# A new order of all steps in a fused attention and feed-forward kernel, with one dummy matmul step fewer

## The chip, the core and the metric

The kernel runs on one core of a Trainium2 chip. The metric is the device time of one execution in microseconds. Times of several executions are compared by their median; the profiles show one execution each.

The core has five engines, each with its own queue[...]: TensorE (PE; its weight loads are shown as PEld), VectorE (DVE), ScalarE (ACT), GpSimd (POOL) and SyncE (SP). POOL and SP also issue the transfers.

## The reference

Eight batches of 8 heads, 576 rows and 64 columns go through an attention with exponential features, then through a Fourier mixing and a feed-forward network.

```python
def phi(x):
    proj = np.einsum('bhsd,df->bhsf', x, w_phi)            # 64 -> 128
    proj = proj - np.max(np.abs(proj), axis=-1, keepdims=True)
    return np.concatenate([np.exp(proj), np.exp(-proj)], axis=-1)
q_p, k_p = phi(q), phi(k)
kv = np.einsum('bhsf,bhsd->bhfd', k_p, v);  z = np.sum(k_p, axis=2)
x = einsum('bhsf,bhfd->bhsd', q_p, kv) / (einsum('bhsf,bhf->bhs', q_p, z)[..., None] + 1e-6)
# heads side by side: x is (8, 576, 512)
mixed = np.real(fft(fft(x, axis=1), axis=2))
u = x + mixed
un = (u - mean(u)) / np.sqrt(var(u) + 1e-6)                # over the 512 columns
out = u + np.maximum(un @ w_ch1, 0.0) @ w_ch2              # 512 -> 2048 -> 512
```

## The kernel before, in words

The work of a batch is cut into *streams*, and each stream into *steps*. A stream is a Python generator; each `yield` ends a step. A string `PLAN` of 1239 letters says which stream takes its next step. Instructions are issued in that order, and each engine works through its own in that order, so the string alone sets the order on all five engines. Nothing is scheduled at run time: an engine waits where the operand of its next instruction isn't ready, and everything behind it waits too.

I name a step by its letter, its batch and its number in the stream, counted from 0: S6.3 is step 3 of stream S for batch 6. The letters are:

- K, V, Q: the loads of k, v and q, issued from POOL (`fetch_k`, `fetch_v`, `fetch_q`). V_b.0 loads the last 64 rows, V_b.1 heads 0 to 3 and V_b.2 heads 4 to 7 into the tile VS, of which there is one. B and A: the transposes of k and q on SP (`arrive_k`, `arrive`).
- T (`steps`): products of keys and of queries with w_phi and their exponentials on ACT. T_b.0 to T_b.8 are for the keys, T_b.9 to T_b.17 for the queries. A product of a key or query step (T_b.9, 11, 14, 16) takes a buffer of the pool `pj`, and its second exponential is made in the step after.
- P (`maxima`): the maxima of the queries. R (`kmax`): those of the keys, on DVE. S (`scaled`): exponentials of these maxima on ACT, then multiplications of V with them on POOL (lines 451 and 466): S_b.0 for the last rows, S_b.1 to S_b.4 for two heads each.
- M (`mixing`): M_b.0 to M_b.7 are the products kv, one head each; M_b.8 to M_b.15 the quotients, one head each, partly on DVE and POOL; M_b.16 to M_b.25 the Fourier transforms. D (`folded`): sums and differences on DVE ahead of these transforms.
- N (`normalise`): the normalised rows UN on ACT, and their transposes UT on SP. U (`scales`): the scale 1/sqrt(var).
- F (`forward`): the feed-forward in 68 steps. A hidden step has four matmuls `psf` (line 1222), an output step two `pso` (line 1239). Two hidden steps of the first 256 rows share one ReLU on ACT (the "paired ReLUs", line 1229); those of the other 320 rows have one each (line 1227).
- W loads the two weights, C, H, Z make constants, and G and J transpose the first batch's k and q on TensorE.
- Y (`stir`): four matmuls of ones whose result nobody reads.

Batch 0 uses the same letters in longer forms (`first_features`, `first_heads`), in which the heads go in pairs 0, 3, 2, 1, and its k and q wait in the space of the weights W2b.

Buffers join the streams. `pj` has two PSUM buffers, shared by T, P (from batch 2 on) and M_b.8 to M_b.20; R reads what T has put there; `pb` has three, shared by F and most of M; `pk` has one, for kv and the dummies. A matmul into a buffer waits until the one before it in that buffer was read.

```python
    with tc.manual_schedule():
        count_first()
        load_first()
        count_rest()
        for name in PLAN:
            step(name)
```

Of the kernel before, what the change touches and what calls it, by code (L numbers as in the profile page):

```python
# [20 lines left out]


PLAN = (
    "YYCCYCYGCGZTGRTGZTZTZRZJQQGSTJRKTPYTSTPRYTWJJJRMPTMTSSMTPPSTPTMTZQMTMMTMPMMVKBTCMTMDTYMVHMYYDYYDDAHM"
    "HYYHTHMMMHKMTTRMNMTMYQNNYVMSNTKNMFFNFNRRFSTPFTPTUFWMNFFMNFFSFRTFVMFFTCURPSYUBNTUTFSUFMFQKTFMFTPPMQTP"
    "VMTFFPUTFUMTMFFAFMMTFFMQFMFDFRFMFTVFFFFRFMFTFFMFFPFFTFFFQDDFFFRFMFTKFFDMTFFFFTFMFFMFRTFMRTFMFSSSSTTM"
    "NPFFTNPBTMMMSMQFTMTPPMFFMFFTMFFFPVTAMFFFPNFFMTFFMNNKUMFFVMMFFQTMFFTFRMRFFTFFFQFMFFMFMFFFPTFFRFFFFDFD"
    "VFTPFFFDFFDKTPRFTFFMMTSFFBFFFMMSSFFMFFRTMTMFFTNMSMFFFTNPPMFMTFFFTMTFSTPMFFFMFFQPFTFMFFVFNMFFFMKTFFAM"
    "NNMFFMFUMFVFFMVQFFMFTTRFFMFFFKFRFFMTQFFFDTMRFFFFFDTPFFFTDDFRPFFFFFMTFTFMFFMFBMRFSSMFFTTTMFMTFFFTFNFN"
    "SFMTTMMFFFPMFTMSTPPMFFSMTFFMNFPFMFFPFFVKMNQKFFMNMUFFMFFMFFVMFAFMFQMFFMFTTRFQRFFFTVFMFFFFDFTPFRFFFPDT"  # L30
    "FFFTFFFDFFFDRTMTMFFFFMBFSMFFSMRFTFTTMSFMFTFNMMMTMFTFFFMNFPSSTMTNFFFFTPPMFFFMFTFPQMFVFKFPFFMFFMANMFFN"
    "FFMKFFMFTUTFMFFRFRFFSVFMFFFFFTMFTFQFRMFDVTFFFMTRFFDFFFFFFFDFFDFTMFTBQFMFFMSFMFRFMFTFTTMFFSMTNFTNFFMP"
    "SMFFMMTFMPTFSMTFFMTPFMFTFFQMFNPPPFVMFFAMFFPFNNUMVFMFTFMFMFFFMFRFFMTRTFSFFFFFPFFMFVFMTFFRFFTFDFDFPTFF"
    "FFDDFRFFTTMMFFFFFFMMFRSFTFFMTFTMTFFNTFSMNFFFMTFTTFMFMFMTSPFMFFFFMFFSMFTPPMFFFMFFMNPFMFFPNNFUMMFFFFMF"
    "FMFFFMMFFFFFFMFFMFFFDFFDFFFDFFDFMFFFFMMFMFMFFFMNMFNFFFFFFFFMMFFFFFFFFFFFFFFFFFFFFNMNFNFFFFFUFFFFFFFF"
    "FFFFFFFFFFFFFFFFFFFFFFFFFFFFFFFFFFFFFFF"
)


# [1 line left out]
def kernel(  # L41
# [11 lines left out]
    B, H, S, D = q.shape  # L53
    DF = w_phi.shape[1]
    C = H * D
# [1277 lines left out]
        return run  # L1333

    def stir(b):
        for i in range(16):
            ps = pk.tile([128, 512], F32, tag="pk", name="idle")
            for x in range(4):
                nc.tensor.matmul(  # L1339
                    ps[:], lhsT=ones_b[:], rhs=ones_b[:].unsqueeze(1).to_broadcast([128, 4, 128]),  # L1340
                    start=True, stop=True,
                )
            yield

    def fold_later(b):
# [4 lines left out]
        "U": (scales, 1), "P": (part(0), 7), "T": (part(1), 18), "R": (part(2), 5),  # L1350
        "S": (part(3), 5), "K": (fetch_k, 2), "V": (fetch_v, 3), "Q": (fetch_q, 3),
        "A": (arrive, 1), "B": (arrive_k, 1), "W": (load_ffn_weights, 2),
        "C": (constants, 6), "H": (sines, 6), "Y": (stir, 16), "G": (turn_first_k, 5), "J": (turn_first_q, 5), "Z": (pads, 6),
    }
    LONGER = {("N", 0): 10, ("U", 0): 7, ("M", 0): 24, ("T", 0): 20}
    at_ = {name: (1 if name in "KVBQA" else 0, 0) for name in STREAMS}
# [51 lines left out]
```

## Time and profile before

| what | value |
|---|---|
| median of 4 runs | 429.64 us (426.75 to 429.8) |
| the profiled execution | 426.75 us |
| its span, first to last instruction | 425.0 us |
| TensorE busy | 402.8 us, 95% |
| VectorE busy | 330.8 us, 78% |
| ScalarE busy | 305.3 us, 72% |
| GpSimd busy | 207.0 us, 49% |
| dummy matmuls (line 1339) | 64, 19.2 us busy |
| first feed-forward matmul | 52.4 us |
| mean granted TensorE clock | 0.999 |

All times within the execution are microseconds from the first instruction. The busy share of TensorE counts overlapping and waiting matmuls, so it is not a share of its peak. In the timeline a row gives start, duration, engine, line, operation, output and inputs; square brackets hold the idle time of the engine ahead of it and what ended that. "PEld ... issue" is time in which nothing that the profile shows was waited for.

### The profile page before, as it was taken

To read this page: it belongs to the slowest core of one execution; us is meant where nothing else is said; L and a number is where in the kernel's file an instruction comes from. 1 tells how busy PE (TensorE), PEld (TensorE's weight loads), DVE (VectorE), ACT (ScalarE), POOL (GpSimd) and SP (SyncE) were. 2 spreads that over 40 slices of the span, in tenths; PEclk is the share of its full clock that TensorE was granted. 3 is DMA by queue.
4 is the path that set the end of the run, shared out by engine and by line. 5 is a ranking of instruction groups with operands and counts; after the bars stand their busy time and mean duration, and the time that the engine had idled before them with its cause. 6 is when DMAs were issued, how large, how long until landed. Compare 5 with 4: busy or idle time off the path is not lost.

```text
span 425.0 us, 10430 instructions
## 1 busy us (share of the span) xinstructions
PE 402.8 (95%) x4126; PEld 255.1 (60%) x4126; DVE 330.8 (78%) x682; ACT 305.3 (72%) x626; POOL 207.0 (49%) x271
## 2 busy tenths in 40 slices
PE   8789789998899999999999999999999999999994
PEld 3465466744676558564675558565856567657562
DVE  4879787899789985998879885998899868965302
ACT  5986899747975889488847997688858785454450
POOL 7992588542965292825574274835554333300100
PEclk9999999999999999999999999999999999999999
DMA  8999979995597945994499259695473141104204
GB/s 218 179 177 160 126 81 163 160 132 105 105 129 80 126 76 80 124 124 77 86 147 140 51 81 133 85 116 106 79 93 49 27 88 32 27 0 79 68 23 86
DMA packets 108699, 42.70 MB, mean 100 GB/s; under 512 B 82859, under 2 KB 103595, under 8 KB 108651
## 3 DMA queue, kind: packets, MB, share of 16 engines
q0 software_dynamic: 45936, 16.60, 37.5%
q1 hardware_dynamic: 62479, 25.31, 32.7%
q8 instruction: 32, 0.52, 0.5%
q10 hardware_dynamic: 236, 0.13, 0.1%
q14 instruction: 16, 0.13, 0.1%
HBM read 36.77 MB, written 9.44 MB: 109 GB/s over the span
## 4 chain that ended last, share of the span: by engine, by line
PE 50%; DVE 31%; ACT 15%; issue 2%; DMA 1%; DVEq 0%; POOL 0%; ACTq 0%; SPq 0%
PE psf L1222 16%; PE pso L1239 13%; DVE cb L999 5%; DVE R L903 4%; DVE MK L511 4%; DVE tg L994 4%; PE kv L887 3%; PE pso L1286 2%; DVE CEO L1034 2%; PE idle L1339 2%; DVE MQ L555 2%; PE pu L1104 2%; ACT KPn L497 2%; DVE rd L1001 2%; DVE X L1245 2%; PE psD L1045 2%
## 5 line engine op out<-in xcount | busy, mean ns | idle before, releaser
L1222 PE MATMUL psf<-UT,W1b 128*128 128x320 bf16 (+1 forms) x1024 | 141.3, 286 | 0.8 <-ACT HT L1229 0.4
L1239 PE MATMUL pso<-W2b,HT 128*128 128x512 bf16 x512 | 125.0, 379 | 0.0
L1222 PEld LDWEIGHTS <-W1b 128*128 128x128 bf16 x1024 | 94.4, 98 | 28.3 <-issue 2.9
L1239 PEld LDWEIGHTS <-HT 128*128 128x128 bf16 x512 | 46.0, 98 | 44.8 <-issue 1.4
L1227 ACT ACTIVATE HT<-psf 128x320 bf16<-128x320 f32 x128 | 53.4, 449 | 24.8 <-PE psf L1222 19.3
L1002 POOL TENSOR_TENSOR X<-cb,rd 128x320 f32<-128x320 f32 x56 | 41.4, 742 | 38.0 <-DVE rd L1001 35.5
L466 POOL TENSOR_TENSOR VCn<-VS,VCn 128x512 bf16<-128x512 bf16 x28 | 29.7, 1060 | 41.6 <-ACT VCn L461 33.3
L1229 ACT ACTIVATE HT<-psf 128x512 bf16<-128x512 f32 x64 | 38.4, 600 | 13.3 <-PE psf L1222 13.0
L555 DVE TENSOR_REDUCE MQ<-psq 128x8 f32<-128x1024 f32 (+1 forms) x32 | 34.2, 1085 | 13.8 <-PE psq L547 13.5
L1245 DVE SCALAR_TENSOR_TENSOR X<-pso,rs,X 128x512 f32<-128x512 f32 x32 | 23.5, 736 | 22.0 <-PE pso L1239 21.9
L497 ACT ACTIVATE KPn<-psk 128x1024 bf16<-128x1024 f32 x28 | 28.5, 1019 | 14.2 <-DVE MK L511 14.0
L497 ACT ACTIVATE KPp<-psk 128x1024 bf16<-128x1024 f32 x28 | 28.7, 1026 | 11.1 <-PE psk L491 11.0
L451 POOL TENSOR_TENSOR V4N<-VS,V4N 64x256 bf16<-64x256 bf16 x14 | 8.8, 631 | 53.2 <-ACT V4N L447 48.3
L1094 DVE TENSOR_TENSOR X<-pu,X 128x512 f32<-128x512 f32 (+3 forms) x49 | 23.5, 529 | 13.8 <-PE pu L1104 13.6
L511 DVE TENSOR_REDUCE MK<-psk 128x8 f32<-128x1024 f32 x28 | 33.7, 1206 | 0.1
L1190 POOL TENSOR_TENSOR rs<-VE,mhalf 128x5 f32<-128x5 f32 (+1 forms) x9 | 10.3, 1143 | 41.1 <-DVE VE L1189 41.0
L466 POOL TENSOR_TENSOR VCp<-VS,VCp 128x512 bf16<-128x512 bf16 x28 | 29.7, 1060 | 0.0
L606 ACT ACTIVATE QPHP<-psh 128x1024 bf16<-128x1024 f32 x28 | 28.8, 1028 | 0.5 <-PE psh L597 0.3
L606 ACT ACTIVATE QPHN<-psh 128x1024 bf16<-128x1024 f32 x28 | 28.9, 1034 | 0.0
L1150 ACT ACTIVATE UN<-X,MV 128x512 bf16<-128x512 f32 (+1 forms) x35 | 24.7, 722 | 5.4 <-issue 2.7
L1174 DVE BATCH_NORM_STATS2 st<-X 128x6 f32<-128x512 f32 (+1 forms) x40 | 27.0, 675 | 0.1
L284 POOL DMA_DIRECT2D QS<-in_q_dram x28 | 23.7, 847 | 3.3 <-DMA QT<-QS 3.2
(465 smaller groups left out, 818.8 us busy)
## 6 DMA issues: line engine op xcount, KB each, us to landing
out_dram<-X SPq DMA_DIRECT2D x16, 256.0 KB
out_dram<-X SPq DMA_DIRECT2D x64, 64.0 KB
QS<-in_q_dram POOLq DMA_DIRECT2D x14, 256.0 KB, 5.7
KS<-in_k_dram POOLq DMA_DIRECT2D x7, 512.0 KB, 6.8
VS<-in_v_dram POOLq DMA_DIRECT2D x14, 256.0 KB, 5.3
W1b<-in_moe_w_ch_dram POOLq DMA_DIRECT2D x1, 2048.0 KB, 13.5
W2b<-in_moe_w_ch_dram POOLq DMA_DIRECT2D x1, 2048.0 KB, 18.3
W2b<-in_k_dram SPq DMA_DIRECT2D x2, 512.0 KB
```

Of the source, the lines that this page charges most:

```text
L466: nc.gpsimd.tensor_tensor(out=VC[:, hs, :, 0:D], in0=values[b][0][:, hs, :].rearrange("p h (j d) -> p h j d", d=D), in1=VC[:, hs, :, D:D + ...
L497: nc.scalar.activation(out=KP[:, hs, :, :].rearrange("p e (jp jj) f -> p jj (e jp) f", jj=2), in_=psk[:], func=AT.Exp, scale=sgn,)
L511: nc.vector.tensor_reduce(out=MK[:, 2 * pr:2 * pr + 2, :].rearrange("p e (jp jj) -> p jj (e jp)", jj=2), in_=tiles[pr][:], axis=AX.X, op=A ...
L555: nc.vector.tensor_reduce(out=o, in_=i[:], axis=AX.X, op=ALU.max, apply_absolute_value=True)
L606: nc.scalar.activation(out=o, in_=psh[:], func=AT.Exp, scale=sgn)
L1002: nc.gpsimd.tensor_tensor(out=X[:, :, D * h:D * h + D], in0=cb[:, :, 0:D], in1=rd[:].to_broadcast([128, 5, D]), op=ALU.mult,)
L1174: nc.vector.bn_stats(out=st[0:M, :], in_=X[0:M, c, 0:C])
L1222: nc.tensor.matmul(ps, lhsT=W1b[:, cc, 128 * hh:128 * hh + 128], rhs=UT[:, cc, lo:hi], start=(cc == 0), stop=(cc == NCC - 1),)
L1227: nc.scalar.activation(out=HT[:, hh, lo:hi], in_=ps, func=AT.Relu, scale=-1.0)
L1229: nc.scalar.activation(out=HT[:, hh - 1:hh + 1, lo:hi], in_=psw[:].rearrange("p (a n) -> p a n", a=2), func=AT.Relu, scale=-1.0,)
L1239: nc.tensor.matmul(po[:], lhsT=HT[:, hh, at:at + 128], rhs=W2b[:, hh, :], start=(hh == 0), stop=(hh == NHH - 1),)
L1245: nc.vector.scalar_tensor_tensor(out=U[:, c, 0:C], in0=po[:], scalar=scale_of[b, c], in1=U[:, c, 0:C], op0=ALU.mult, op1=ALU.add,)
```

## The change

The order of all steps is replaced by another one, found by a new search; the streams and their instructions stay the same. Stream Y has 15 steps instead of 16, so 60 dummy matmuls instead of 64. The letters in `PLAN` are 1238.

```diff
 PLAN = (
-    "YYCCYCYGCGZTGRTGZTZTZRZJQQGSTJRKTPYTSTPRYTWJJJRMPTMTSSMTPPSTPTMTZQMTMMTMPMMVKBTCMTMDTYMVHMYYDYYDDAHM"
-    "HYYHTHMMMHKMTTRMNMTMYQNNYVMSNTKNMFFNFNRRFSTPFTPTUFWMNFFMNFFSFRTFVMFFTCURPSYUBNTUTFSUFMFQKTFMFTPPMQTP"
-    "VMTFFPUTFUMTMFFAFMMTFFMQFMFDFRFMFTVFFFFRFMFTFFMFFPFFTFFFQDDFFFRFMFTKFFDMTFFFFTFMFFMFRTFMRTFMFSSSSTTM"
-    "NPFFTNPBTMMMSMQFTMTPPMFFMFFTMFFFPVTAMFFFPNFFMTFFMNNKUMFFVMMFFQTMFFTFRMRFFTFFFQFMFFMFMFFFPTFFRFFFFDFD"
...
+    "CCZCYYZYGGCTZVTRZKGTGRZWGJTTSJYRSJTQTTPPYTYRPTJMRJTMSMMSPSTKPTPTZMYTMMQTMTPMCQTMMTMTBDMHKMHKHDDHYAHY"
+    "DYMYMHYTMMVMRTQMTNMMYTNTQNNYSFNMFNFNRVRFSTTPTFMFRSYUNTFWMURFVFFFFUUMTPMFBSTFMNTUTPNUSMFVPPCTFMFTUPQM"
+    "TFMFTFPATVMFFFMMFTFMFKMFFMQFMFRTKFMFFRFPFDFFFFTFFFFTDFFFDRTFFFMFFTTDMFRFFFFSFFMFFFTFMSMFRFTMTTNMTFMN"
+    "FPTMMFFSMTPMFTPPMTFFFMFFQNMPTFBSFMFFQMFFPTFFMNNUAMFFMFMFVTRTFFMFFVRVFFKMFKFFFFTMFMFFFFQMFPFDFFTPFRFF"
...
     def stir(b):
-        for i in range(16):
+        for i in range(15):
             ps = pk.tile([128, 512], F32, tag="pk", name="idle")
...
-        "C": (constants, 6), "H": (sines, 6), "Y": (stir, 16), "G": (turn_first_k, 5), "J": (turn_first_q, 5), "Z": (pads, 6),
+        "C": (constants, 6), "H": (sines, 6), "Y": (stir, 15), "G": (turn_first_k, 5), "J": (turn_first_q, 5), "Z": (pads, 6),
```

Four places of which the prediction speaks, written out in steps (before, then after):

```
ahead of the first kv:  S0.0 T0.4 J0.1 R0.2 K1.0 T0.5 P0.0 Y0.4 T0.6 S0.1 ... Y0.5 T0.8 W0.0 J0.2 J0.3 J0.4 R0.4 M0.0 P0.2 T0.9
                        S0.0 J0.1 Y0.3 R0.2 S0.1 J0.2 T0.5 Q1.0 ... Y0.4 T0.8 Y0.5 R0.3 P0.2 T0.9 J0.3 M0.0 R0.4 J0.4 T0.10
batch 2, end of keys:   M1.20 R2.4 T2.8 F0.63 M1.21 F0.64 S2.0 S2.1 S2.2 S2.3 T2.9 T2.10 M1.22 N1.0 P2.1 F0.65 F0.66 T2.11
                        S2.0 ... M1.18 ... S2.1 M1.20 F0.62 R2.4 F0.63 T2.8 M1.21 T2.9 T2.10 N1.0 M1.22 T2.11 F0.64 M1.23 N1.1 F0.65 P2.1 T2.12
batch 6, V:             V6.2 M5.15 ... S6.1 ... S6.2 ... S6.3
                        S6.1 ... S6.2 M5.23 M5.24 M5.25 M6.0 V6.2 T6.13 F4.64 F4.65 S6.3 M6.1 T6.14 P6.1 M6.2 S6.4
batch 5, K and S4:      S4.3 T4.16 ... S4.4 ... V5.0 ... K6.0
                        M4.0 B5.0 S4.3 F2.63 K6.0 T4.13 T4.14 M4.1 Q5.1 ... S4.4
```

More of the change, by code (lines that the diff above doesn't have):

```diff
@@ L23 @@
 PLAN = (
-    "YYCCYCYGCGZTGRTGZTZTZRZJQQGSTJRKTPYTSTPRYTWJJJRMPTMTSSMTPPSTPTMTZQMTMMTMPMMVKBTCMTMDTYMVHMYYDYYDDAHM"
-    "HYYHTHMMMHKMTTRMNMTMYQNNYVMSNTKNMFFNFNRRFSTPFTPTUFWMNFFMNFFSFRTFVMFFTCURPSYUBNTUTFSUFMFQKTFMFTPPMQTP"
-    "VMTFFPUTFUMTMFFAFMMTFFMQFMFDFRFMFTVFFFFRFMFTFFMFFPFFTFFFQDDFFFRFMFTKFFDMTFFFFTFMFFMFRTFMRTFMFSSSSTTM"
-    "NPFFTNPBTMMMSMQFTMTPPMFFMFFTMFFFPVTAMFFFPNFFMTFFMNNKUMFFVMMFFQTMFFTFRMRFFTFFFQFMFFMFMFFFPTFFRFFFFDFD"
-    "VFTPFFFDFFDKTPRFTFFMMTSFFBFFFMMSSFFMFFRTMTMFFTNMSMFFFTNPPMFMTFFFTMTFSTPMFFFMFFQPFTFMFFVFNMFFFMKTFFAM"
@@ L29 @@
[L29 to L33, printed above, removed]
@@ L34 @@
-    "FFDDFRFFTTMMFFFFFFMMFRSFTFFMTFTMTFFNTFSMNFFFMTFTTFMFMFMTSPFMFFFFMFFSMFTPPMFFFMFFMNPFMFFPNNFUMMFFFFMF"
-    "FMFFFMMFFFFFFMFFMFFFDFFDFFFDFFDFMFFFFMMFMFMFFFMNMFNFFFFFFFFMMFFFFFFFFFFFFFFFFFFFFNMNFNFFFFFUFFFFFFFF"
-    "FFFFFFFFFFFFFFFFFFFFFFFFFFFFFFFFFFFFFFF"
+    "CCZCYYZYGGCTZVTRZKGTGRZWGJTTSJYRSJTQTTPPYTYRPTJMRJTMSMMSPSTKPTPTZMYTMMQTMTPMCQTMMTMTBDMHKMHKHDDHYAHY"
+    "DYMYMHYTMMVMRTQMTNMMYTNTQNNYSFNMFNFNRVRFSTTPTFMFRSYUNTFWMURFVFFFFUUMTPMFBSTFMNTUTPNUSMFVPPCTFMFTUPQM"
+    "TFMFTFPATVMFFFMMFTFMFKMFFMQFMFRTKFMFFRFPFDFFFFTFFFFTDFFFDRTFFFMFFTTDMFRFFFFSFFMFFFTFMSMFRFTMTTNMTFMN"
@@ new lines @@
+    "FPTMMFSSMTPMFTPPMTFFFMFFQNMPTFBSFMFFQMFFPTFFMNNUAMFFMFMFVTRTFFMFFVRVFFKMFKFFFFTMFMFFFFQMFPFDFFTPFRFF"
+    "FTFDPFFTFFDDFFRFFTMFFFTMFFMMBSFFMSFRFTMMTFTNNFMFMMMKFTFMTSTFFFFSMPPTMTFFFFFMFSFMFPTMQQVFFFPTKFFMNNNM"
+    "FFMFFMFFUMFFMFMFFFAMTRTVFFRTVFFFFFQMFFFDFDFTFFFDRFTPDFFFTPFFRFFTMFFFFTMMMFSFFRSFTMFTFMTTFNFTFMFNSMMM"
+    "FMBSFKTTMQNFFFNPFMTFFFMFTPPFMFSFMNFPQMUTFVFKFPAFFMMFMFFVMFFMTFMFFMFFFMRTFRVFFTFFFQMFFFFTDDFRFFFFTFDP"
+    "FFDFTPFFFRFTMTFFFFFMMMFFRFSFSTMSTFFMTFTFFNMFFTNMMMMSTTFMFFQNFTFPMFFFMFVNFMTBPPFSFMFFTPFMKFFFMFFQPNMF"
@@ L37 @@
+    "FMAUKFFMFFFMTTFRFRFMFFFTSFFFFVTMFFFRMTQFFFMTFFFFDFDFFFRFDFTFFDMFTFMFFMFSMFMRFTFFTMFTFTFFTMNNFPSMMMMV"
+    "TFFSMTPMSTQFFMTPMFTFBQMFPPPFFMFFMFNVFPFFANNUMFFMFMTFMFFMFFMFFRTFRMFFFFFFFVTTPFSFFRFVFFMTFDFFTFFFDFDR"
+    "FFFFFTDMTMFFFFFMMFFSFRFTMFTTTMNFMTNMFFFFMSFMMPSTFMFFFNFPTMFFFFFFMTPPSFMFFMFPTFMFFPNFFTMFNMFFMFMFFUFM"
+    "FMFFFFMMFFFFFFMFFFFDFFFDFDFFFDFMFFMFFMFFMMFFMNMFFNFFFFFFMFMFMFFFFFFFFFFFFFFFFFFFNFFFFFNFNFFFUFFFFFFF"
+    "FFFFFFFFFFFFFFFFFFFFFFFFFFFFFFFFFFFFFF"
 )
```

## The prediction

> **What bounds the kernel now.** I read the page first, for the busy shares.
>
> ```profile
> PE 402.8 (95%) x4126; PEld 255.1 (60%) x4126; DVE 330.8 (78%) x682; ACT 305.3 (72%) x626; POOL 207.0 (49%) x271
> ```
>
> TensorE seems full, but this share also counts matmuls that wait, as the windows (PE, PEld, DVE, ACT, POOL busy us of 10, with the instructions in brackets) show:
>
> ```profile
> 10.00:20.00 10.00, 7.91 (x85) 5.11 (x84) 8.79 (x12) 9.88 (x19) 9.69 (x15) 1.00 1.11 201
> ...
> 90.00:100.00 10.00, 10.00 (x61) 4.59 (x60) 9.93 (x23) 5.85 (x9) 1.50 (x2) 1.00 0.82 117
> 100.00:110.00 10.00, 7.52 (x72) 4.03 (x71) 8.94 (x16) 8.95 (x22) 5.95 (x8) 1.00 0.43 84
> ```
>
> From 10 to 20 us ACT and POOL are full and TensorE is not; from 90 to 100 ACT has 4 us free; from 100 to 110 it is nearly full and TensorE loses 2.5 us. For the price of a matmul without waits I took the chain that ended last, at its end:
>
> ```profile
> 386.74 6.68 PE psf L1222 x60
> ...
> 394.29 6.91 PE pso L1239 x32
> 401.20 8.69 PE psf L1222 x64
> 409.89 6.91 PE pso L1239 x32
> ```
>
> So one psf matmul is 0.111 us (256 columns) or 0.136 (320), and one pso 0.216. The feed-forward has 512, 512 and 512 of these, 237 us, and with the rows of 64 tokens about 252. Pricing every other matmul by the shortest pitch of its row in the timeline, I get 359 us of useful TensorE work and 14 of dummies (64 x 0.216). Laid against the time at which each step ran, the 425 us leave 22 us lost in the first 70 us, 23 from 70 to 418 (some 7 in waits over 0.2 us, the rest at changes from one kind of matmul to another), and 7 after the last matmul. Only the 23 us and the front can be won or lost by an order.
>
> **The change part by part.** It moves steps and removes one dummy step. I summed, in the order of each string, the durations that each step has in this trace, up to the same milestones. At M_b.16 (b = 1 to 7) the DVE sums of the two orders differ by at most 1.2 us and the ACT sums by at most 1.0, one instruction each. So this is the same schedule with local swaps; I cost the swaps that I found to matter.
>
> *Dummy.* 15 groups of four instead of 16. A warm group is 4 x 0.216 = 0.86 us. Three instead of four stand ahead of the first transposes:
>
> ```profile
> 1.12 1.90 PE idle L1339 x4
> ...
> 6.91 1.21 PE idle L1339 x4
> 8.12 0.40 PE pst L368 x4
> ```
>
> The transposes begin as the fourth group ends, and their data had landed by about 6 us, so they start up to 1.2 us earlier. ACT takes little of that: it is busy until 7.3 us, and C0.3 now stands behind G0.1. Bounds -0.9 and 0; I take 0 and let the next item hold the front. The first row (0.47 us per matmul against 0.216) shows a slow TensorE until about 7.3 us. [...] By the row nothing is lost: the dummies still end near 6.9, and transposes follow. [...]
>
> *Front, batch 0.* On POOL the order ahead of S0.1 was Q1.0, Q1.1, K1.0 (1.14 + 0.90 + 0.72 = 2.76) and is V1.0, K1.0, W0.0 (1.28 + 0.72 + 0.82 = 2.82); two memsets (1.06) move into its wait ahead of C0.3's last operation, so S0.1 ends up to 1 us earlier. Q1.0 (1.14) now stands between S0.1 and S0.2, which eats that. P0.2 and T0.9 go ahead of M0.0, which removes 0.7 us of DVE idling and the 0.4 of ACT. Against this the exponentials of S0.3 stand behind M0.3's copy on ACT:
>
> ```profile
> 24.98 1.06 POOL L869 TENSOR_TENSOR VCn<-HT,VCn 128x512 bf16<-128x512 f32 x1 [0.85 <-ACT VCn L862]
> ```
>
> I put it at 25.4 instead of 24.98. S0.4, M0.6, M0.7 and P0.6's transpose follow it one after the other, and from P0.6 on DVE works without a pause up to M0.17. So +0.4, with -0.9 (the gains arrive) and +1.0 (ACT also waits for R0.2 in S0.1) as bounds. K2.1 now waits on POOL for the transposes of KS, with H0.4 behind it, which M0.16 needs; by the present times it is free near 41 us and H0.4 ends at 42.1 now, so nothing. Without that cover H0.4, and M0.16 with it, would slip as far as K2.1 does. W1 is loaded 4 us earlier and is needed only at 52.
>
> *The ACT jam of batch 2.* This is the largest single wait after the start:
>
> ```profile
> 103.46 0.44 ACT L447 ACTIVATE V4N<-MK 64x4 bf16<-64x4 f32 x2
> ...
> 104.85 1.00 ACT L606 ACTIVATE QPHP<-psh 128x1024 bf16<-128x1024 f32 x1
> ...
> 106.82 0.39 PE L597 MATMUL psh<-QT,wphi 64*128 64x512 bf16 x2 [1.62 <-ACT QPHN L606]
> ...
> 109.60 0.28 PE L576 MATMUL ph<-QT,wphi 64*128 64x256 bf16 x2
> ```
>
> The psh at 106.82 is T2.11. It needs a buffer of pj (there are two) that T2.9 holds until ACT has made both exponentials; ahead of these stand S2.0, S2.1 and S2.3, from 103.46 to 104.85: 1.4 us. ACT has no gap from 101.5 to 109.8. In the new order S2.0 and S2.1 come before M1.18 and M1.20, where ACT idles, and S2.3 after T2.12; and T2.11 takes the buffer of M1.20, free since 102.3. P2.1 takes its place in the wait, and then T2.13, which needs T2.12: 109.8 - 1.4 = 108.4 instead of 109.6, with F0.67 (0.44) still to do. That is -0.8, and half of the next two waits (0.36 and 0.51 us in the timeline, ahead of M2.1 and P2.4) makes -1.2; bounds -2.2 and 0.
>
> *Smaller waits after 112 us.* Those over 0.2 us sum to about 4, the largest 1.0 ahead of M2.20 for DVE. DVE has the same work before it, TensorE 0.5 us more cover: -0.4 in all, bounds -1.5 and +1.0.
>
> *Changes of stream on TensorE.* In the strings, 486 before and 477 after. A change from one kind to another costs 0 to 0.2 us in the timeline; nine at 0.1 is -0.9, of which half falls where TensorE waits anyway: -0.4, bounds -1.0 and 0.
>
> *V6.2.* The second half of batch 6's V is issued on POOL behind S6.2 instead of ten us before S6.1:
>
> ```profile
> 277.82 0.81 POOL L284 DMA_DIRECT2D VS<-in_v_dram  x1
> ...
> 288.02 1.05 POOL L466 TENSOR_TENSOR VCn<-VS,VCn 128x512 bf16<-128x512 bf16 x1 [6.68 <-ACT VCp L461]
> ...
> 296.15 1.06 POOL L466 TENSOR_TENSOR VCn<-VS,VCn 128x512 bf16<-128x512 bf16 x1 [4.03 <-ACT VCn L461]
> ```
>
> Of the V loads, the view of the tile VS says:
>
> ```profile
> DMA to landing us min/median/max: 2.3/5.0/15.9
> ```
>
> S6.1 and S6.2 are four multiplications, 288.0 to 292.1; V6.2 then lands at 297.1 by the median, S6.3 ends at 299.2 and S6.4 at 301.3. M6.4 needs S6.3 at about 299.8 and M6.6 needs S6.4 at 303.5. A landing of 5.0 us is just hidden: +0.1, bounds 0 and +4. Queued behind S6.3 on POOL are S6.4 and Q7.1; behind M6.4 on TensorE is everything.
>
> *Other loads.* They are issued earlier or land in time by the durations here. The nearest case is K6.0, which waits on POOL for SP's transposes of B5.0, now right ahead of it and behind those of N3.0 and N3.1 (issued at 203.0 and 204.4, 1.2 to 1.7 us each): free near 208, then K6.0 0.7, Q5.1 0.9 and S4.4 2.1 end at 212, and M4.6 comes at about 212.4. Hidden by the four kv steps M4.2 to M4.5 and the F steps between; 0, bounds 0 and +1.
>
> *The end.* From M7.16 the two orders differ by single steps; F7.0 keeps 13 F steps between N7.1 and itself and gains M7.25. Nothing.
>
> Sum: 0 + 0.4 - 1.2 - 0.4 - 0.4 + 0.1 + 0 = -1.5 us. The profiled execution took 426.75 (span 425.0); 425.25 then. The median of the four runs is 429.64, 2.9 above it, and I carry that over: 428.1.
>
> **The rivals.** About 0.5%, 2.15 us, is what a measurement of this kernel can tell from no change: below 427.5 is faster, above 431.8 slower.
>
> *All covers work* (chance 0.22): jam -2.2, front -0.9, half of the smaller waits more, -1.3 in all, gives 429.64 - 4.4 = 425.2. For it: ACT has 4 us free right before the jam. Against: DVE is 9.93 of 10 full there and has the same sum.
>
> *V6.2 decides, slower* (0.13): its place is S6.3, its price every microsecond that the landing exceeds about 5.6. The column of landings has 15.9 at its end, and K4.1, issued at 134.6, landed after 10 us. At 10 us M6.4 waits 4.4 us; the rest of the sum (-1.6) stays: 432.4. Against: the W2 load made the 15.9, and is long over.
>
> [...]
>
> *The order doesn't do what it says* (0.13): the swaps are no better than chance and new small waits of buffers appear; 0 to +3, about 431.5.
>
> **How the numbers follow.** The main case has 0.45 and spans 426.5 to 430.2. Faster: 0.10 of it and 0.20 of the first rival, 0.30. Slower: V6.2 0.13, cold array 0.06, the last rival 0.07, 0.26. The rest, 0.44, is within the bound. The range 425.2 to 433.8 leaves about one in ten out on each side.
>
> **What would show it.** Right: no wait over 0.5 us at T2.11; L447 of batch 2 before 101 us; the window of the jam with over 8.5 us of TensorE; the first psf within 1 us of 52.4. Wrong: a wait of POOL for the DMA of VS near 292 to 300 with TensorE idle at the kv after it (V6.2); matmuls of 0.43 us pitch after 8 us (cold); P0.6 over 1 us later; or new waits of TensorE over 1 us elsewhere that no item names.

## The result and the profile after

The changed kernel takes 426.64 us (median of 41 runs, 425.69 to 428.81), the kernel before 428.75 us beside it (62 runs, 426.33 to 430.27). The ratio is 0.996, 95% interval 0.9949 to 0.997: 0.4% less, which is no more than the 0.5% that a measurement of this kernel can tell from no change. A second set gave 0.998 (0.9965 to 0.9995). The profiled execution took 426.67 us (span 424.9), where that of before took 426.75. So two profiles that differ by nothing stand for medians that differ by 2 us; most of what follows is about that.

The page of after, its busy shares and the granted clock in 40 slices of the span:

```profile
PE 400.8 (94%) x4122; PEld 255.7 (60%) x4122; DVE 329.9 (78%) x682; ACT 306.1 (72%) x626; POOL 207.3 (49%) x271
...
PEclk9899999999999999999999999999999999999999
```

Work and shares are the same. New is the 8 in the second slice: TensorE was granted less than its full clock there. The windows of after (columns: PE, PEld, DVE, ACT and POOL busy us, then the granted clock):

```profile
10.00:20.00 10.00, 7.11 (x66) 3.76 (x64) 9.06 (x12) 9.30 (x17) 9.61 (x15) 0.86 1.04 202
...
90.00:100.00 10.00, 10.00 (x63) 4.57 (x60) 9.93 (x21) 6.21 (x12) 2.51 (x4) 1.00 0.37 61
100.00:110.00 10.00, 8.83 (x93) 4.68 (x91) 8.92 (x18) 9.19 (x19) 4.70 (x5) 1.00 0.59 105
```

From 100 to 110 us TensorE is busy 8.83 us instead of 7.52, which is the jam of batch 2 made smaller. From 10 to 20 the clock is 0.86. The timeline of TensorE shows where:

```profile
17.16 0.58 PE L749 MATMUL psq<-wphi,QT 64*128 64x128 bf16 x7 [0.39 <-DVE MQ L755]
17.67 3.41 PE L1339 MATMUL idle<-ones_b 128*128 128x512 bf16 x8
21.02 0.41 PE L766 MATMUL psq<-wphi,QT 64*64 64x128 bf16 x8
```

Eight dummies (Y0.4 and Y0.5) take 3.41 us where eight at full clock take 1.73 (0.216 each): the granted clock is 0.50 from 17.1 to 20.6 us and 1.00 on both sides.

The jam, in the timelines of ACT and TensorE of after:

```profile
96.95 0.45 ACT L447 ACTIVATE V4N<-MK 64x4 bf16<-64x4 f32 x2
...
103.48 0.93 PE L597 MATMUL psh<-QT,wphi 64*128 64x512 bf16 x4
...
108.66 0.28 PE L576 MATMUL ph<-QT,wphi 64*128 64x256 bf16 x2 [0.76 <-DVE MQ L555]
```

S2.0's exponentials (L447) run at 96.95 instead of 103.46. T2.9 and T2.11 now stand in one row of four matmuls (0.93 us, where two take 0.39 and two more at 0.111 would make 0.61: 0.3 us of waiting), and the wait of 1.62 us is gone. T2.13 starts at 108.66 instead of 109.60.

The front is late, though. The first psf starts at 53.6 us where it was 52.4, and the reason is on POOL and ACT:

```profile
25.81 1.06 POOL L869 TENSOR_TENSOR VCn<-HT,VCn 128x512 bf16<-128x512 f32 x1 [1.46 <-ACT VCn L862]
```

S0.3 starts 0.83 us later than the 24.98 of before. And behind 150 us there are waits that before did not have, of the first F step of a batch for its transposed rows:

```profile
158.70 1.03 PE L1222 MATMUL psf<-UT,W1b 128*128 128x256 bf16 x8 [0.56 <-DMA UT<-UN]
...
205.36 1.36 PE L1222 MATMUL psf<-UT,W1b 128*128 128x256 bf16 x11 [0.61 <-DMA UT<-UN]
...
252.81 1.38 PE L1222 MATMUL psf<-UT,W1b 128*128 128x256 bf16 x11 [0.79 <-DMA UT<-UN]
```

Priced step by step as in the prediction, after has done 1.3 us less useful TensorE work than before at 70 us, and ends 0.1 us ahead: the part behind 70 us gained 1.4. Nearly all of that was gained before 112 us. When F1.0 starts, both orders have put the same matmuls on TensorE but for the one dummy step, and its first psf stands in before and in after at

```profile
111.72 0.49 PE L1222 MATMUL psf<-UT,W1b 128*128 128x256 bf16 x3
```

```profile
111.70 0.49 PE L1222 MATMUL psf<-UT,W1b 128*128 128x256 bf16 x3
```

So what the front lost is made up by then, and all that lies behind gained 0.1 us (0.2 in the profile of after_again).

### The profile page after: what moved, and what is told of

It reads as the page before. It is cut to its first block, busy times and chain, and to the rows that moved or that the text cites. A ratio compares the mean times of both kernels' runs of the same rounds, so it can differ in the third digit from the quotient of the medians.

```text
span 424.9 us, 10423 instructions
## 1 busy us (share of the span) xinstructions
PE 400.8 (94%) x4122; PEld 255.7 (60%) x4122; DVE 329.9 (78%) x682; ACT 306.1 (72%) x626; POOL 207.3 (49%) x271
## 4 chain that ended last, share of the span: by engine, by line
PE 58%; DVE 26%; ACT 10%; DMA 3%; issue 2%; POOL 0%; DVEq 0%; ACTq 0%
PE psf L1222 19%; PE pso L1239 18%; DVE R L903 4%; DVE cb L999 3%; PE idle L1339 3%; PE kv L887 3%; DVE tg L994 3%; DMA UT<-UN 2%; DVE MK L511 2%; PE psD L1045 2%; DVE CEO L1034 1%; DVE X L1094 1%; PE pu L1104 1%; PE pso L1286 1%; DVE MQ L555 1%
## 5 line engine op out<-in xcount | busy, mean ns | idle before, releaser
L1239 PEld LDWEIGHTS <-HT 128*128 128x128 bf16 x512 | 46.4, 98 | 46.5 <-issue 2.6
L1245 DVE SCALAR_TENSOR_TENSOR X<-pso,rs,X 128x512 f32<-128x512 f32 x32 | 23.6, 736 | 24.3 <-PE pso L1239 24.3
L987 PEld LDWEIGHTS <-QPHP 128*128 128x128 bf16 x280 | 21.2, 99 | 4.6 <-DVE cb L999 1.0
```

Of the source, the lines that this page charges most:

```text
L1239: nc.tensor.matmul(po[:], lhsT=HT[:, hh, at:at + 128], rhs=W2b[:, hh, :], start=(hh == 0), stop=(hh == NHH - 1),)
```

## The experiments

Three theories stood before the first set of runs. *Order*: the gain comes from the order behind 70 us. *Dummy*: it comes from the dummy step that was left out. *Clock*: the times of before lie in two bunches (29 of the 62 runs at 426.3 to 428.2, 33 at 428.6 to 430.3, nothing between), a half-clock stretch in the sparse first 30 us makes the upper one, and the change alters how often that falls on work that matters.

All runs were compared with before in the same set. The sets ran on different chips. Since the median of before hangs on how many runs fall into its upper bunch, the last column gives this median less that of before's lower bunch (runs under 428.5) in the set.

| run | median us (range, runs) | before | ratio (95%) | less lower bunch |
|---|---|---|---|---|
| after, first set | 426.64 (425.69-428.81, 41) | 428.75 | 0.996 (0.9949-0.997) | -0.8 |
| before_less_dummy | 428.05 (426.56-429.82, 22) | 427.79 | 0.9995 (0.9977-1.0013) | +0.7 |
| after_more_dummy | 427.86 (426.77-429.53, 14) | 427.79 | 0.9996 (0.9977-1.0016) | +0.5 |
| front_before_rest_after | 427.36 (425.44-429.61, 14) | 427.79 | 0.9969 (0.9945-0.9993) | 0.0 |
| front_after_rest_before | 430.35 (428.95-431.83, 9) | 427.79 | 1.0053 (1.003-1.0076) | +3.0 |
| after_again | 427.22 (426.21-428.54, 22) | 427.50 | 0.998 (0.9965-0.9995) | +0.2 |
| before_filled | 427.35 (426.52-428.42, 22) | 427.50 | 0.9986 (0.9971-1.0) | +0.3 |
| joined_filled | 425.70 (425.02-426.58, 10) | 427.50 | 0.9947 (0.9925-0.9969) | -1.3 |
| after_filled | 426.64 (425.28-428.06, 22) | 427.50 | 0.9967 (0.995-0.9984) | -0.4 |
| before_filled_jam | 426.97 (426.14-427.91, 21) | 427.90 | 0.9972 (0.9957-0.9987) | -0.2 |
| joined_filled_no_jam | 427.89 (427.09-428.59, 14) | 427.90 | 0.999 (0.9972-1.0009) | +0.7 |
| after_filled_less_mid | 427.24 (426.21-428.32, 22) | 427.90 | 0.9981 (0.9967-0.9996) | 0.0 |
| joined_filled_early_n | 426.23 (424.20-427.88, 20) | 427.90 | 0.9946 (0.9929-0.9962) | -1.0 |

One execution of before_filled_jam, of 1381 us, is left out of its range and count here.

**The dummy.** One alone is taken out of before, and one put back into after:

```diff
 before_less_dummy:  - Y0.3 ahead of G0.0        (16 -> 15 dummy steps, order of before)
 after_more_dummy:   + a fourth Y ahead of G0.0  (15 -> 16 dummy steps, order of after)
```

> The kernel before with nothing changed but the fourth early dummy step (Y0.3, four matmuls just ahead of G0.0) left out: the dummy alone. Theory 'order' (what the change gains comes from the order of the steps after 70 us): the dummy is worth nothing, 428.7 us, ratio 1.000 +/- 0.001. Rival 'dummy' (the 0.87 us of four warm matmuls come straight off the start): 427.9, ratio 0.998. Rival 'clock' (the runs of before lie in two bunches, 427.3 and 429.5, because a half-speed window of 3.4 us falls into the sparse first 21 us in some executions): with one dummy fewer the array is warm as soon or later and goes cold at least as often, 428.7 to 430, ratio 1.000 to 1.003.

> The changed kernel with a fourth dummy step put back ahead of G0.0 (16 in all): the new order without the dummy's removal. 'Order': as the changed kernel, 426.6 us, ratio to before 0.995. 'Dummy': 427.5, ratio 0.997. 'Clock': one dummy more makes the half-speed window rarer by a little at most, 426 to 426.6, ratio 0.994 to 0.995.

Without the dummy before stays as it is (0.9995), and 10 of its 22 runs lie at 428.5 and above, as 20 of the 46 runs of before do. So the dummy's removal does not take the upper bunch away. A small gain is not excluded: the runs under 428.5 have a median of 427.0 where those of before have 427.4, and the others 429.3 where those of before have 430.0, 0.4 and 0.6 of the 0.87 us that "dummy" named. after_more_dummy came to +0.5 us against the lower bunch, which fitted none of the three; after_again, at +0.2 in the next set, lies within its interval. One thing about it stands out: 4 of its 14 runs took 428.5 us or more, where after has 3 of 63. Its profiled execution (428.77 us) has half clock from 49.1 to 52.5 us and its first psf at 54.4 us, where after has 53.6:

```profile
49.08:52.50 3.42, 3.42 (x15) 1.60 (x17) 2.55 (x11) 2.44 (x3) 0.00 (x0) 0.50 1.64 162
```

Whether the added dummy brings that on, 14 runs don't tell; "clock", which expected it to become rarer, is not borne out here.

**The two halves.** The order of one kernel up to S1.1 (about 57 us), that of the other behind it:

```diff
 front_before_rest_after:  steps up to S1.1 in before's order, then the steps left in after's
 front_after_rest_before:  steps up to S1.1 in after's order, then the steps left in before's
```

> The order of before up to S1.1 (about 57 us), then the order of after for all that is left; the two prefixes differ by M0.23 and Q2.1 alone. 'Order': at 70 us the traces show before 1.3 us of TensorE work ahead of after, and after makes up 1.4 us behind that; together the two halves give 425.3 us, ratio 0.992. 'Clock' (the front decides between the two bunches of before): 428 to 428.7, ratio 0.998 to 1.000, in two bunches like before.

> The order of after up to S1.1 (about 57 us), then the order of before. 'Order': after's front is 1.3 us behind in the profiled executions and nothing is made up, 429 to 430 us, ratio 1.001 to 1.003. 'Clock': after's front spares the slow bunch, 426.5 to 427.5, ratio 0.995 to 0.997.

front_before_rest_after reaches 425.44, lower than any run of before (426.29) or after (425.69), but 6 of its 14 runs lie at 427.9 to 429.6. Both theories are right in part: the rest of after is about 1.4 us better (the eight other runs, at a mean clock of 0.992 and more, have a median of 426.0, before's lower bunch 427.4), and the front of before brings the upper bunch with it. front_after_rest_before is 3.0 us behind before's lower bunch, more than "order" allowed (1.3) and far from the gain that "clock" said. Its T2.11 still waits 1.61 us, as in before. In its profile the first psf stands at 54.5 us, 2.1 behind before: 1.2 of that is the late front of after, and the other 0.9 comes with a half-clock stretch from 43.1 to 46.5 us (six psD take 1.29 us from 45.38 on and 0.75 from 46.67 on). Why the rest is as large was not settled.

**Where the clock comes in.** The profiled execution of before_less_dummy fell into the upper bunch (429.41 us). Its granted clock on the page, and its windows:

```profile
PEclk9969999999999999999999999999999999999999
```

```profile
20.14:23.55 3.41, 1.91 (x37) 1.31 (x37) 2.28 (x4) 2.10 (x7) 3.32 (x4) 1.00 0.35 49
23.55:26.97 3.42, 3.42 (x39) 2.38 (x40) 2.11 (x6) 1.76 (x7) 2.65 (x3) 0.50 1.05 206
26.97:30.37 3.40, 3.40 (x46) 2.61 (x40) 2.32 (x6) 2.51 (x6) 3.40 (x7) 0.50 1.07 213
```

TensorE was busy 1.91 us of 3.41 and then had half clock for two stretches of 3.41 us, which is where the queries and kv of batch 0 are made one after another. The eight psn of T0.12 in the timeline of before_less_dummy:

```profile
25.73 1.03 PE L697 MATMUL psn<-mt,pick 96*128 96x128 bf16 x8
```

and in that of before:

```profile
25.61 0.62 PE L697 MATMUL psn<-mt,pick 96*128 96x128 bf16 x8
```

The profile of front_before_rest_after has the same two stretches at the same place, and its first psf at 54.5 us where joined_filled, below, has it at 51.9: 2.6 us, the distance of the two bunches (429.6 against 427.0 in the set of after_again). The half clock of 6.83 us is 0.008 of the mean clock over 427.6 us, so 0.999 becomes 0.991. And the clock is recorded with each run: of the 174 runs of before in the three sets, 76 took 428.5 us or more, and every one of these had a mean clock of 0.992 or less; of the 98 faster ones 10 had. No execution of before itself was profiled in the upper bunch; that its half clock falls in the same place is read from the two kernels that share its front.

To test this, idle stretches were filled with dummies:

```diff
 before_filled:  J0.4 + Y ... T0.10 + Y          (order of before, 18 dummy steps)
 joined_filled:  the same two in front_before_rest_after
 after_filled:   G0.4 + Y ... T0.5 + Y ... Y0.9 + Y   (order of after, 18 dummy steps)
 after_again:    after, unaltered
```

> The changed kernel once more, unaltered, beside the runs of this set. Expected from its first set: 426.6 us, the fastest near 425.7, ratio 0.996; if the new order on its own is worth less than the first set showed (the run with the dummy put back came to 427.9), 427.5 or more, ratio 0.998 to 1.000.

> The kernel before with two dummy steps more, one behind J0.4 and one behind T0.10: there its TensorE stood idle 1.08 and 0.97 us in the profiled execution, and each step takes some 0.9 us. 'Clock' (a half-speed window falls at 23.5 to 30 us in the executions of 428.6 us and more, because TensorE is busy too little in the 3.4 us ahead of it): the upper bunch is gone, all runs at 426.5 to 428, median 427.2, ratio 0.997, mean granted clock never below 0.991. Rival (the two bunches come from elsewhere, a DMA or the start): both bunches stay, each later by nothing to 1 us, ratio 1.000 to 1.002.

> The order of before up to S1.1 and that of after behind it (which gave 425.44 to 429.61), with the same two dummy steps behind J0.4 and T0.10. 'Clock': the upper part of its runs (427.9 to 429.6, all at a granted clock of 0.987 to 0.991) is gone, 425.5 to 427, median 425.9, ratio 0.993 to 0.994, which beats both kernels. Rival (bunches from elsewhere): as without them, 427.4, ratio 0.997 to 0.999.

> The changed kernel with three dummy steps more, behind G0.4, T0.5 and Y0.9, where its TensorE stood idle 1.06, 1.23 and 1.80 us in the profiled execution. 'Clock': the runs of 427 and more go, 425.7 to 426.6, median 426.0, ratio 0.993 to 0.995. 'Dummy' (in this order a dummy more costs its own time, as the one put back ahead of G0.0 seemed to, about 1 us each): 427.5 to 429, ratio 0.998 to 1.002.

The window of 20 to 24 us in before_filled:

```profile
20.00:24.00 4.00, 3.79 (x46) 2.04 (x45) 3.28 (x5) 3.07 (x9) 3.98 (x5) 1.00 0.62 64
```

and in before:

```profile
20.00:24.00 4.00, 2.14 (x39) 1.40 (x38) 3.27 (x5) 3.07 (x9) 3.98 (x5) 1.00 0.58 67
```

TensorE is busy 3.79 us of 4 instead of 2.14, and the other engines are not touched. The upper bunch is gone: none of 22 runs reaches 428.5, beside 26 of 63 of before. The lower bunch did not get faster (+0.3). The interval of the ratio ends at 1.0, but the missing bunch doesn't rest on it. joined_filled did the same and more: 425.02 to 426.58, ratio 0.9947 against 0.998 for after_again in the same set. It beats both kernels (its slowest run is faster than 17 of the 22 of after_again), and has 18 dummy steps instead of 15. after_filled gained little over after_again (426.64 against 427.22, overlapping intervals); "a dummy more costs its own time" is out, and after had no upper bunch to lose.

**The jam.** The stretch from F0.50 to P2.6 (about 95 to 115 us) of after is put into before_filled, and that of before into joined_filled:

```diff
 before_filled_jam:     ... S2.0 ... M1.18 ... S2.1 M1.20 ... T2.9 T2.10 N1.0 M1.22 T2.11 ... P2.1 T2.12 ... S2.2 S2.3 ...
 joined_filled_no_jam:  ... F0.64 S2.0 S2.1 S2.2 S2.3 T2.9 T2.10 M1.22 N1.0 P2.1 F0.65 F0.66 T2.11 ...
```

> The filled kernel before (before_filled: 426.5 to 428.4, median 427.35), with the stretch from F0.50 to P2.6 (about 95 to 115 us) in the order of after and everything else in that of before: the prediction's largest term alone. If that term holds (1.2 us between 102 and 110 us): 426.15, ratio 0.995 to 0.996 where before_filled had 0.9986. Rival (the gain behind 57 us is spread over many small waits and the stretch gives a third or less of it): 427.0 to 427.4, ratio 0.998 to 0.999.

> The joined and filled kernel (425.02 to 426.58, median 425.7), with the stretch from F0.50 to P2.6 put back to the order of before. If the term of 1.2 us holds: 426.9, ratio 0.997 to 0.998. Rival (spread): 425.7 to 426.1, ratio 0.994 to 0.996.

before_filled_jam stands at -0.2 us against the lower bunch where before_filled stood at +0.3: about 0.6 us gained with more digits, half the term, but no more than the intervals of the two ratios leave open. joined_filled_no_jam stands at +0.7 where joined_filled stood at -1.3: 2.0 us lost, more than the term, and here the intervals do not meet. In its timeline the old wait is back:

```profile
106.50 0.39 PE L597 MATMUL psh<-QT,wphi 64*128 64x512 bf16 x2 [1.65 <-ACT QPHN L606]
```

So the jam is a real cause. What is left of it at the end seems to hang on its neighbours, though 0.6 and 2.0 are not clear of each other by these intervals. In joined_filled_no_jam the stretches over 0.2 us behind 70 us in which TensorE stands idle sum to 6.9 us, where joined_filled has 4.8; the old wait is 1.65 of that, and others follow from it. In before_filled_jam the 10 us ahead of it pay for part of the gain (columns as above):

```profile
90.00:100.00 10.00, 9.20 (x57) 3.94 (x56) 9.93 (x23) 6.75 (x15) 3.34 (x5) 1.00 0.76 110
100.00:110.00 10.00, 8.74 (x87) 4.46 (x87) 8.85 (x16) 8.75 (x19) 5.76 (x6) 1.00 0.57 102
```

From 90 to 100 TensorE is busy 9.20 instead of the 9.94 of before_filled, while from 100 to 110 it is 8.74 instead of 7.50. And it waits 0.71 us at 207 and 0.41 us at 254 us for UT, where before_filled has 0.23 us at 254.

**The dummy in busy time.** After runs Y0.6 at 28.2 us, where before has no dummy between 20 and 33 us:

```diff
 after_filled_less_mid:  M0.4 - Y0.6 T0.14   (the rest as after_filled)
```

> The changed kernel with its three idle stretches filled (after_filled: 425.28 to 428.06, median 426.64), and the dummy step that it runs at 28.2 us between M0.4 and T0.14 left out; before had none between 20 and 34 us, where its TensorE is busy 0.95 and more, so this one dummy was moved from idle time into busy time. If that is what puts after's front behind: 0.9 us less, median 425.7, first psf near 52.7 us, ratio 0.993 to 0.995. Rival (VectorE's chain sets the front, the dummy lies in its shadow): 426.6, first psf at 53.6 us, ratio 0.996 to 0.998.

The rival was right. In the timeline the dummy's time turned into a wait:

```profile
29.93 0.29 PE L887 MATMUL kv<-VCp,KPp 128*128 128x65 bf16 x4 [0.80 <-DVE ml L731]
```

This is M0.6, at 29.93 us without the dummy and at 29.97 in after with it. The DVE operation named ends at 29.90, but M0.6 reads nothing of it; it reads what S0.4 multiplies on POOL, and that ends at 29.88 (29.84 in after_filled, 29.92 in after). First psf, in the source view of after_filled_less_mid:

```profile
L1222 PE MATMUL psf<-UT,W1b x1024: 269/290/311, 53.6 to 410.4; 128*128 128x320 bf16 x86, 128*128 128x256 bf16 x85
```

53.6, as in after: the dummy doesn't set the front. By these rows POOL's S0.3 and S0.4 do, where the expectation named VectorE. But VectorE is close behind. P0.6's transpose also reads m, whose last operation in before and in after is

```profile
29.45 0.18 DVE L733 TENSOR_TENSOR m<-ml,m 128x20 bf16<-128x20 f32 x1
```

```profile
30.79 0.18 DVE L733 TENSOR_TENSOR m<-ml,m 128x20 bf16<-128x20 f32 x1
```

It ends 1.34 us later, 0.48 us ahead of the transpose (31.45 in the timeline of TensorE). So an earlier S0.3 alone could win about 0.4 us at P0.6 unless this chain came earlier with it; the order of S0.3 by itself was not tried.

**The new waits for UT.**

```diff
 joined_filled_early_n:  N3.3 ahead of F2.64, N4.2 ahead of F3.64 (the rest as joined_filled)
```

> The joined and filled kernel with N3.3 moved ahead of F2.64 and N4.2 ahead of F3.64, two or three steps earlier, so that the transposing loads of UT for F3.0 and F4.0 are issued earlier; its TensorE waited 0.48 us at 203 and 0.84 us at 251 us for these. If the waits go and nothing else comes: 424.5 to 425, ratio 0.991 to 0.993. Rival (the gain is given back at the next late step of VectorE): 425.5 to 426, ratio 0.994 to 0.995.

No gain shows: -1.0 us against the lower bunch where joined_filled had -1.3, although its fastest run, 424.20, is the lowest of all. Its profiled execution (427.58) is one of its two slowest: half clock from 47.7 us on (mean clock 0.993) puts its first psf at 53.3, where joined_filled has 51.9. The timeline has the waits still there:

```profile
204.51 1.47 PE L1222 MATMUL psf<-UT,W1b 128*128 128x256 bf16 x12 [0.63 <-DMA UT<-UN]
...
253.42 1.48 PE L1222 MATMUL psf<-UT,W1b 128*128 128x256 bf16 x12 [1.02 <-DMA UT<-UN]
```

They are 0.63 and 1.02 us where joined_filled had 0.32 and 0.68. An earlier step in the order doesn't make its data earlier. UN of N4.2 (251.32 us) starts 0.04 us after the end of the VectorE result that it reads (line 1175), as it does in joined_filled (249.54, 0.03 after).

## Why the prediction was right, and where it was not

The time (426.64 in the first set, 427.22 in the second) lies in the range 425.2 to 433.8, and "within 0.5%" was the likeliest. The central value, 428.1, was 1.5 high, and two of its steps were wrong in ways that cancelled in part, so that it came so near is partly luck: the change in the profile was said to be -1.5 and was -0.1, and the 2.9 us put on top of it did not belong there. Of its own signs, the three of the jam came true and the fourth did not: the first psf is 1.2 us late, and P0.6 over 1 us later (1.19) was on its list of signs of being wrong.

*The dummy, 0:* right within what could be told. Taken from the middle of after_filled it made nothing better (0.0 against the lower bunch, where after_filled has -0.4). Taken out of before it may be worth 0.4 to 0.6 us in each bunch, inside the bounds of -0.9 and 0. Put back into after it left 4 of 14 runs at 428.5 and above, which was not followed up.

*The front, +0.4:* the term of the sum that was mis-sized; it measured +1.2 at the first psf. The gain on POOL ahead of S0.1 did not come: C0.3's last operation itself came at 10.44 instead of 9.68, and S0.1 at 19.29 instead of 19.20. I put S0.3 at 25.4 on POOL; it came at 25.81. The copies of M0.1, M0.2 and M0.3 stand ahead of its exponentials on ACT, and M0.2's product can't start before POOL ends S0.2 at 24.3; in before S0.3 went ahead of M0.2 and had its exponentials out by then. I had counted M0.3 only. That is 0.83, of which 0.75 is left at M0.7; another 0.3 to 0.4 comes from T0.15, which now stands between M0.6 and P0.6 on TensorE (VectorE's own chain into P0.6 is late as well, as shown above). P0.6's row on DVE came at 31.74 instead of 30.55, and DVE carried this 1.2 us through to the end of batch 0's Fourier steps, as the prediction had said it would. The half clock is not the cause: in after_filled, at a mean clock of 0.998, P0.6's row is at 31.66. Bound of the term was +1.0, too narrow.

*K2.1 on POOL, nothing:* right by its own test. It waited 8.1 us for the transposes of KS and went out at 42.29. H0.4 ends at 44.04 instead of 42.08, 2.0 us later, but the cover was just enough: M0.16 starts at 44.48, 1.2 us later than before, and so does M0.15 ahead of it, which needs nothing of H0.4.

*The jam, -1.2:* the mechanism was right, and the 1.2 us that the front lost are made up by F1.0. T2.11's wait went from 1.62 to 0.3 us, L447 came before 101, and TensorE was busy over 8.5 us in the window, the three signs named. T2.13 came at 108.7 with a front 1.2 us late, where 108.4 was said. By itself it came to 0.6 in one surrounding and 2.0 in the other; 1.2 lies between.

*Smaller waits, -0.4, and changes of stream, -0.4:* the 1.0 us wait ahead of M2.20 (0.86 in the brackets) is gone, but three waits of 0.56 to 0.79 us for UT have come, which no item named (the prediction had set 1 us as the sign of such waits). By the idle times that the timeline puts in brackets, the stretches over 0.2 us sum to 3.2 us behind 112 us where before has 1.9 (the prediction, counting otherwise, had put them at about 4), and to 1.2 from 70 to 112 us where before has 2.7. So behind the jam they grew, where the term had them shrink, which was the step that failed here; that the end still came 0.1 us ahead must lie in shorter losses, which were not traced one by one. With the jam and V6.2 these terms were to give -1.9 behind 70 us; -1.4 was measured there, nearly all of it ahead of 112 us.

*V6.2, +0.1:* right. POOL issued it at 292.48 (the prediction had 292.1), it landed 5.0 us later, at 297.50, and S6.3 started at 297.64, as the exponentials on ACT that it also reads ended. TensorE did not wait for it. The rival of a slower kernel was not tested: this load took less than 5.6 us in the profiled execution, and no run delayed it.

*Sum, -1.5:* in the profiled executions it was -0.1, front +1.3 and the rest -1.4.

*"The median of the four runs is 2.9 above it, and I carry that over":* the step that failed most. The 2.9 us are no constant offset. The profiled execution of before was one of its lower bunch, three of the four shown runs were of its upper one, and the difference is the half clock at 23 to 30 us (by the two profiles of kernels with its front, and by what filling the gap did). After has next to no upper bunch (1 of 41 runs over 428.5, then 2 of 22), so its median is that of its profile, 426.64 beside 426.67. Against before's lower bunch alone after is between 0.8 faster and 0.2 slower, which is the -0.1 of the profiles within what the sets can tell. Of the 2.1 us of the first set, 1.3 are the upper bunch that went away: the median of before is 428.75, that of its lower bunch 427.44.

*The chance of 0.06 for a "cold array", slower:* no run shows this term, which was the author's estimate. Its sign, matmuls of 0.43 us pitch after 8 us, came (eight dummies in 3.41 us), but the half clock fell in both orders, and with TensorE at work: the stretches of 3.4 us ahead of it were busy 45 to 60% (see the last section). In after it falls at 17.1 to 20.6 us on two dummy steps and costs nearly nothing (S0.3 on POOL at 25.81, against 25.73 in after_filled without it). In front_before_rest_after, with the front of before, and in before_less_dummy, one dummy step short of that, it falls at 23.6 to 30.4 us on the densest part of batch 0, and the upper runs of before, some 2.5 us longer, have a mean clock of 0.992 or less. So it was looked for in the right place, with the wrong sign.

## What to carry to other kernels

Ask for the spread of the times and for the granted clock of each run before an offset between a profile and a median is carried over: two bunches that differ in the clock (here 0.992 or less in all 76 runs of the upper, in 10 of the 98 of the lower) are two kinds of execution, and a change may do no more than move runs from one to the other. Ahead of a dense stretch of TensorE, fill idle time with dummies where TensorE waits anyway: in before_filled two of them took away the 2.5 us that 4 runs in 10 of before had on top. Look at all runs afterwards, though: one dummy put back at the start of after may have moved a half-clock stretch onto the work ahead of the feed-forward. An order that a search found as a whole doesn't come apart freely: joined with those of another its two halves were 1.3 us better (gaps filled) and 3 us worse, and one rearranged stretch came to 0.6 us here and 2.0 there.

## What the runs showed of the hardware

TensorE fell to half clock behind stretches in which it was busy 45 to 60%. The 3.41 us ahead of a fall, as long as the half clock of after, in the windows of after, and of joined_filled (which fell where it cost little):

```profile
13.73:17.14 3.41, 1.65 (x30) 1.14 (x30) 2.62 (x5) 3.29 (x10) 3.41 (x6) 1.00 1.10 209
17.14:20.55 3.41, 3.34 (x14) 1.27 (x14) 2.98 (x4) 3.02 (x4) 3.11 (x5) 0.50 1.00 167
```

```profile
11.58:14.99 3.41, 2.05 (x24) 1.15 (x23) 2.78 (x4) 3.31 (x9) 3.40 (x6) 1.00 0.95 291
14.99:18.40 3.41, 3.41 (x24) 1.36 (x21) 3.25 (x5) 3.38 (x7) 3.17 (x6) 0.50 1.63 186
```

TensorE was busy 48% and 60% of the windows ahead, in after with no pause over 1.23 us. In before the window ahead of the dense part was 61% busy and nothing fell:

```profile
20.97:24.39 3.42, 2.09 (x43) 1.49 (x43) 2.66 (x5) 2.49 (x7) 3.14 (x4) 1.00 0.54 89
```

No clean limit follows. Nine of the fourteen profiles have a fall to half clock before the last matmul, and the 3.4 us ahead of it were busy 45% (front_after_rest_before, 1.54 of 3.40 us) to 60% (joined_filled). But stretches as sparse stayed at full clock: the last matmuls of before (1.75 us of 3.42 from 416.91 on, 51%) and of after (2.06 of 3.42 from 416.49 on, 60%), and two in after_more_dummy (56% and 47%):

```profile
14.90:18.40 3.50, 1.96 (x28) 1.18 (x28) 2.81 (x5) 3.40 (x10) 3.35 (x6) 1.00 1.17 154
38.80:42.30 3.50, 1.64 (x7) 0.67 (x7) 3.46 (x11) 2.01 (x5) 0.17 (x1) 1.00 0.94 194
```

What decides is not the busy share alone; whether the size or kind of the matmuls matters was not tried. Nor is it the order alone. The half clock begins at 17.14 us in after and at 17.58 in after_again, the same program. It begins at 14.55 us in before_filled_jam and at 14.99 in joined_filled, and before_filled, which has the same order up to 57 us, was at full clock from 13 to 31 us, with a mean clock of 0.998. In after the first stretch at full clock is 10.24 us long and the half-clock one 3.41, a third of it. That the moment of the fall is what puts executions of the same program in either bunch is the author's estimate, from these times; what sets the moment was not shown.
